# Three small moves in an attention and expert kernel: a row sum with its diagonals, a token list, and the last copy

## The chip, the cores and the metric

The kernel runs on one core of one Trainium2 chip. A core has TensorE (PE in the profile, with its weight loads as PEld), VectorE (DVE), ScalarE (ACT), GpSimd (POOL) and SyncE (SP); each works through its own queue of instructions in order, and they wait for one another by semaphores. TensorE writes its products to PSUM, a small memory in banks, from which VectorE and ScalarE read them. The metric is the device time of one execution in microseconds; the median over runs counts.

## The reference

First an attention block in the manner of RWKV5 (batch 4, 8 heads, 768 positions, head dimension 48), then a layer of 8 experts to which tokens are assigned greedily and in equal numbers.

```python
for t in range(S):
    kt, vt, rt = (k[:, :, t], v[:, :, t], r[:, :, t])
    cur = np.einsum('bhd,bhe->bhde', u[None] * kt, vt)
    y[:, :, t] = np.einsum('bhd,bhde->bhe', rt, state + cur)
    state = w[None, :, :, None] * state + np.einsum('bhd,bhe->bhde', kt, vt)
...
x = y.transpose(0, 2, 1, 3).reshape(3072, 384)
logits = x @ w_gate
for idx in np.argsort(-logits.flatten()):
    tok, e = idx // E, idx % E
    if assigned[tok] < 0 and counts[e] < 384:
        assigned[tok] = e
        counts[e] += 1
for e in range(E):
    out[assigned == e] = np.maximum(x[assigned == e] @ w1[e], 0) @ w2[e]
```

The weights of an expert are 384 x 1024 and 1024 x 384; everything is float32.

## The kernel before

**The attention** (class `Mild`) is cut into N = 24 units, four batches times six chunks of 128 positions; unit n is batch n mod 4, chunk n div 4. Its order is written out by hand in `Mild.run`, whose body for n finishes unit n and prepares the units after it; every engine receives its instructions in that order. For one unit the steps are these:

- `own(n)`: GpSimd multiplies r, k and u to `rk` (L442, L443).
- `own_sum(n)`: VectorE sums `rk` over the head dimension to `dd`, one number for a position and a head (L448).
- `turn(n)`: TensorE turns keys and r (L458); ScalarE copies the keys (`kT`, L475), VectorE scales r (`rT`, L477).
- `diagonal(n)`: ScalarE writes the eight heads' `AT` as the identity times `dd`, eight instructions at L495. They fill the diagonal and clear the rest.
- `pairs(n)`: TensorE multiplies `kT` by `rT` into the one buffer `g_ps` (L504); VectorE copies the part off the diagonal over `AT` with a mask, in two instructions, one for each half of the heads (L508). The buffer is free again after the second.
- `outputs(n)`: TensorE adds the state's part (`rT` by `states`) and the unit's own part (`AT` by `vts`) into the one buffer `y_ps` (L542); ScalarE copies it to `x` (L561).

In the body for n, `outputs(n)` and `pairs(n + 1)` belong to different units, and `diagonal(n + 2)` and `own_sum(n + 2)` to a third. Rows of x go back to memory by `rows_turned` (TensorE, L592; in the body for 23 it reuses the buffer of `g_ps`), `xr` (ScalarE, L601) and a transfer on SP's queue. In between, the steps of `walk.early` (names with `e_`) choose one expert, called the star, in advance from the chunks that are done, and list 256 of its tokens: `e_some`, `e_part`, `e_both` on VectorE, `list_ps` on TensorE (L1427), `e_tok` on VectorE, and then two gathers by GpSimd (L1515).

**The experts** (class `Experts`) follow, one after the other, numbers 0 (the star's first 256 tokens) to 8 (the star's last 128). For each, `walk` finds by search which expert fills next and which tokens it takes, `tokens` turns the places into a list of token numbers (VectorE makes `row`, `oh` and `vals`; TensorE six `some_ps`, L1409; VectorE `some`, `part`; TensorE `list_ps`, L1427; VectorE `mine`, `tok`), and `fetch` gathers rows and loads weights. The generator `later` holds this work, cut into slots by `yield`. `Experts.run` pulls the next slots at the progress marks in `due`: up to 1 is the first product of the expert, from 1 to 2 the second. Here a scheduler decides the final order, which is the same on every execution.

Some experts (3, 6 and 7) form the first product by seven smaller products P1 to P7 instead of eight (`hidden_by_seven`, L1598), in two passes. Sums of weights (`first_T`, L1545) and of rows (`first_S`, L1556) go in; VectorE adds `kept_P` to a product's bank (L1590), ScalarE keeps banks as `kept_P` (L1582) and writes `hid` (L1586). P6's bank is used again by P7 once ScalarE has kept it. Experts 6 and 7 form the second product by fifteen products (`p_ps`, L1726) from sums of `hid` and weights (`H`, `W`, L1670), with output sums on VectorE (L1735).

**The end.** Expert 8's output is a single block of 128 rows. `result` copies it from PSUM to `o_last` and its tokens to `tok_last`, since another arm of the program, which is not executed with these inputs, ends in the same tiles. After it each engine loads the flag `ok` (L975), branches (L1970), raises its count, and GpSimd scatters `o_last` to the output (L1747), called from the function's last line.

Of the kernel before, what the change touches and what calls it, by code (L numbers as in the profile page):

```python
# [274 lines left out]
class Mild:  # L275
# [340 lines left out]
    def run(self, step):  # L616
        N, B, C, walk = self.N, self.B, self.C, self.walk
        self.live = {n: {} for n in range(N)}
        self.start()
        u_ps = self.spread_u()  # L620
        self.again_one(0, 0)
        k0 = self.keys_turned(0, True)
        self.again_one(0, 1)
        self.idle(2, "g_ps")
        r0 = self.r_turned(0)
        self.copy_u(u_ps)
        self.own(0)
        self.scaled(0, "k", k0, "pieces")
        self.scaled(0, "r", r0, "pieces")
        self.table(self.WK, "k")  # L630
        self.again_one(1, 0)
        self.table(self.WR, "r")
        self.again_one(1, 1)
        self.idle(2, "g_ps")
        k1 = self.keys_turned(1, True, walk.ps, "few")
        wk_ps = self.wk_turned()
        r1 = self.r_turned(1, walk.ps, "counts")
        self.wk_table(wk_ps)
        self.scaled(1, "k", k1, self.WK)
        self.own_sum(0)  # L640
        self.diagonal(0, (0,))
        self.again_one(2, 0)
        self.diagonal(0, (1,))
        self.again_one(2, 1)
        self.scaled(1, "r", r1, self.WR)
        self.own(1)
        self.keys(0)
        self.own_sum(1)
        nc, AB = self.nc, self.ones8
        nc.vector.tensor_mul(self.chunk, AB[:, 0, :, 1, 8], AB[:, 0, :, 1, 8])  # L650
        self.pairs(0)
        self.diagonal(1)
        self.own(2)
        chores = walk.constants()
        for n in range(N):
            self.load(n + 5, "kr")
            self.load(n + 4, "v")
            if n == 2:
                self.gate_weights()
            soon, split, full = n <= B, 0 < n < 3, n >= B and n % B == 0  # L660
            halves = ((0,), (1,)) if split or full else ((0, 1), ())
            if n == 0:
                self.turn(2, True)
                self.own_sum(2)
                self.idle(3, "y_ps")
                self.pairs(1)
                self.keys(1)
            else:
                step(n, "first")
                if not soon and n + 3 < N:  # L670
                    self.again(n + 3)
                if n == 2:
                    self.own_sum(n + 2)
                if split:
                    self.keep(n - 1)
                    self.pairs(n + 1)
                if n + 2 < N:
                    if n != 2 and n + 3 < N:
                        self.own_sum(n + 2)
                    self.turn(n + 2, between=lambda: step(n, "turning"))  # L680
                if n <= N - B:
                    self.rows((n - 1,), "few")
            if soon:
                self.again_one(n + 3, 0)
            if n + 2 < N:
                self.diagonal(n + 2, halves[0])
            if soon:
                self.again_one(n + 3, 1)
            if n > 2:
                step(n, "turned")  # L690
                if n <= B:
                    self.keep(n - 1)
                if n + 1 < N:
                    self.pairs(n + 1, lambda: step(n, "products"))
                step(n, "paired")
            if n + 3 < N:
                self.keys(n + 3)
                self.own(n + 3)
                if n == 1:
                    self.keys(2)  # L700
            if full:
                self.gate(n // B - 1, range(B))
                if n + 2 < N:
                    self.diagonal(n + 2, halves[1])
            if n == N - 1:
                rows = self.rows_turned((N - 4, N - 3), "g_ps", lambda: step(n, "rows"))
                self.rows_out((N - 4, N - 3), rows)
            self.outputs(n, lambda: step(n, "states"), (lambda: self.logits(n // B - 1)) if full else (lambda: None))
            if split:
                self.diagonal(n + 2, halves[1])  # L710
            if n == N - 4:
                self.own_sum(N - 1)
            step(n, "last")
            if n == 13:
                walk.guess_most(self.LG[:, 0:3 * B, :], AX.XY)
            if n == 14:
                walk.guess(walk.ps.tile([128, 128], F32, name="most_ps", tag="few"), self.ident)
            if n == N // 2 + 1:
                for _ in chores:
                    pass  # L720
                self.test()
            if n > 2:
                for _ in range(6):
                    next(chores, None)
        self.gate(C - 1, range(B - 1))
        one = self.rows_turned((N - 2,), "kT_ps")
        self.gate(C - 1, [B - 1])
        last = self.rows_turned((N - 1,), "g_ps")
        self.logits(C - 1)
        return one, last  # L730
# [719 lines left out]
def rwkv5_eagle_then_base_layer_balanced(  # L1450
# [12 lines left out]
    nc = tc.nc  # L1463
    N, DX = out.shape
    E, _, F = moe_w1.shape
# [12 lines left out]
    walk = Assignment(ctx, tc, LG, CAP, C)  # L1478
    out_rows = dram_disjoint_views(out, NT)
    o_last = keep.tile([128, DX], F32, name="o_last")  # L1480
    tok_last = keep.tile([128, 1], I32, name="tok_last")
# [3 lines left out]
    class Experts:  # L1485
# [252 lines left out]

        def leave(self, o_sb, tok, to):
            if to is None:  # L1740
                nc.scalar.copy(o_last, o_sb)
                nc.vector.tensor_copy(tok_last, tok)
            else:
                self.scatter(o_sb, tok, to)

        def scatter(self, o_sb, tok, to):
            nc.gpsimd.indirect_dma_start(out=to, out_offset=bass.IndirectOffsetOnAxis(ap=tok, axis=0),  # L1747
# [2 lines left out]
        def result(self, c, hid, w2, tok, to):  # L1750
            o_ps = self.ps_o.tile([128, DX], F32, name="o_ps")
            for j in range(KF):
                nc.tensor.matmul(o_ps, hid[:, j, ts(c, 128)], w2[:, j, :], start=(j == 0), stop=(j == KF - 1))  # L1753
            if to is None:
                nc.scalar.copy(o_last, o_ps)
                nc.vector.tensor_copy(tok_last, tok[:, c:c + 1])
                return
            o_sb = self.o.tile([128, DX], F32, name="o_sb")
            nc.scalar.copy(o_sb, o_ps)
            self.scatter(o_sb, tok[:, c:c + 1], to)  # L1760
# [3 lines left out]
        def run(self, ahead, later, rows, pulls={}, xT=None):  # L1764
            xT, lead = xT or self.turn(ahead), True
            row_sums = weight_sums = None
            while ahead:
                n, _, tok, w1, w2 = ahead
# [8 lines left out]
                right = (self.fifteen_w2 if many else self.seven_w2)(w2) if whole and not late else None  # L1777
                left = {}
                some = pulls.get(n, 2)
                due = [1.55, 1.75] if some == 2 else [0.75 + 1.15 * i / (some - 1) for i in range(some)]  # L1780

                def half(hid):
                    nonlocal right
# [79 lines left out]
    with ExitStack() as whole:  # L1863
        x = Experts()
# [5 lines left out]
        with ExitStack() as part:  # L1870
# [20 lines left out]
            with tc.manual_schedule():  # L1891
# [18 lines left out]
                tok = walk.tokens(first["place"])  # L1910
# [15 lines left out]
                for m in (0, 1, 99):  # L1926
                    go(m)
                    xT = next(turned)
# [3 lines left out]
        def later():  # L1932
            yield from search
            walk.bound(ident)
            now = second
            for n in range(2, 5):
                walk.book(now, first=True)
                yield x.fetch(n, now["fmax"], walk.tokens(now["place"]))
                walk.leave(now)
                yield  # L1940
                now = walk.new_outs()
                yield from walk.likely_steps(**now)
            was = now
            walk.book(was)
            walk.leave(was)
            for n in range(5, E):
                rest = n == E - 1
                yield
                if rest:
                    yield  # L1950
                    now = walk.remainder()
                else:
                    now = walk.new_outs()
                    yield from walk.likely_steps(**now)
                walk.book(now, surely=rest)
                walk.choose(was, now)
                yield x.fetch(n, was["fmax"], walk.tokens(was["place"]))
                if not rest:
                    walk.leave(now)
                was = now  # L1960
            yield
            yield
            tc.mark_branch_hint_location("whole")
            have["ok"] = walk.found()
            yield x.fetch(E, walk.star, walk.tokens(walk.star_place, 1))

        x.run(ahead, later(), (a for a in [*out_rows[2:NT - 1], None]),
              {1: 5, 2: 7, 3: 9}, xT)

    with tc.If(have["ok"] < 1, label="whole", preferred_fallthrough_block=False):  # L1970
        with ExitStack() as arm:
# [2 lines left out]
        with ExitStack() as arm:  # L1974
            x = Experts()
# [40 lines left out]
```

## Time and profile before

| | us |
|---|---|
| median of 3 runs | 395.65 (395.48 to 396.61) |
| the profiled execution, its own time | 395.83 |
| its span, first to last instruction | 394.1 |
| TensorE's granted clock | 0.998 |

| engine | busy, us | share of the span |
|---|---|---|
| TensorE | 381.2 | 97% |
| VectorE | 281.3 | 71% |
| ScalarE | 169.1 | 43% |
| GpSimd | 141.0 | 36% |

The attention lasts until about 130 us, the experts from there to the end. In a line of the timeline the first number is the start in us from the span's start, the second the length (of several instructions, where it ends in xN with N over 1), then engine, line of the kernel, operation, output<-input, sizes. In square brackets stands how long the engine had been idle before it and what released it. A wait for several semaphores is put down to the one that came last by the profile, and that need not be the one that the program names.

### The profile page before, as it was taken

The page shows a single profiled execution, that of the slowest core. Times are in us where ns is not written, and L with a number is a line of the kernel's source. Part 1 is how long each engine was busy: PE and PEld are TensorE (multiplying, and loading weights), DVE is VectorE, ACT ScalarE, POOL GpSimd, SP SyncE. Part 2 cuts the span into 40 slices and gives each one's busy share as a digit, 9 for nine tenths or more (in the row PEclk, how much of TensorE's full clock was granted, in tenths as well). Part 3 has the DMA queues.
Part 4 walks back from the last instruction along what each step waited for, and adds up shares of the span by engine and source line. Part 5 has one row for each costly group of instructions (what it writes and reads, how often), then busy time and mean ns, then how long its engine had stood idle before and what let it go on. Part 6 is the DMA issues. An engine that isn't in the chain of part 4 may idle for free. (4 is left out here: it accounts for less than half of the span.)

```text
span 394.1 us, 9090 instructions
## 1 busy us (share of the span) xinstructions
PE 381.2 (97%) x3393; PEld 309.5 (79%) x3393; DVE 281.3 (71%) x959; ACT 169.1 (43%) x452; POOL 141.0 (36%) x173
## 2 busy tenths in 40 slices
PE   8999999999999999999999999999999999999993
PEld 7778888888887766677568799558756889989991
DVE  6855777576786778986859949978378976994530
ACT  4997878788883411222222242121222233234130
POOL 7888877656742013032121121202303202070020
PEclk9999999999999999999999999999999999999999
DMA  9999999987592155461470470109209265181010
GB/s 120 160 182 172 197 196 182 171 175 146 113 360 78 58 188 231 145 237 42 119 280 22 132 290 20 41 2 339 83 20 318 97 214 194 38 331 33 2 62 27
DMA packets 95332, 57.30 MB, mean 145 GB/s; under 512 B 77232, under 2 KB 89520, under 8 KB 95280
## 3 DMA queue, kind: packets, MB, share of 16 engines
q1 hardware_dynamic: 91936, 47.21, 47.7%
q0 software_dynamic: 3104, 9.44, 6.9%
q8 instruction: 28, 0.46, 0.5%
q14 instruction: 24, 0.20, 0.2%
q10 hardware_dynamic: 240, 0.00, 0.0%
HBM read 47.20 MB, written 9.44 MB: 144 GB/s over the span
## 5 line engine op out<-in xcount | busy, mean ns | idle before, releaser
L1621 PE MATMUL h_ps<-xT,w 128*128 128x384 f32 (+1 forms) x264 | 72.6, 427 | 0.0
L495 ACT ACTIVATE AT<-ident,dd 128x128 f32<-128x128 f32 x192 | 59.7, 394 | 1.2 <-DVE dd L448 1.1
L1621 PEld LDWEIGHTS h_ps<-xT,w 128*128 128x128 f32 x264 | 42.0, 191 | 19.6 <-issue 2.2
L1515 POOL DMA_INDIRECT xg<-x_rows,tok x22 | 22.2, 1008 | 92.3 <-PE h_ps L1621 23.7
L1747 POOL DMA_INDIRECT out_dram<-o_all,to x16 | 20.8, 1301 | 85.8 <-DVE o_all L1735 22.2
L508 DVE COPY_PREDICATED AT<-mask,g_ps 128x512 f32<-128x512 uint8 x48 | 32.7, 733 | 13.1 <-PE g_ps L504 11.5
L1624 ACT ACTIVATE hid<-h_ps 128x384 f32<-128x384 f32 (+1 forms) x40 | 17.9, 449 | 54.2 <-PE h_ps L1621 50.9
L1753 PE MATMUL o_ps<-w,hid 128*128 128x384 f32 x96 | 32.5, 490 | 0.0
L504 PE MATMUL g_ps<-rT,kT 48*128 48x128 f32 x384 | 27.9, 284 | 1.0 <-ACT x L561 0.6
L436 POOL TENSOR_TENSOR kss<-krs,wk 128x384 f32<-128x384 f32 x24 | 24.3, 1014 | 8.0 <-DVE krs L340 5.2
L504 PEld LDWEIGHTS g_ps<-rT,kT 48*128 48x128 f32 x384 | 23.4, 187 | 4.3 <-ACT AT L495 0.9
L1753 PEld LDWEIGHTS o_ps<-w,hid 128*128 128x128 f32 x96 | 17.7, 190 | 10.6 <-issue 0.5
L542 PE MATMUL y_ps<-AT,vts 128*64 128x128 f32 x384 | 25.7, 276 | 0.0
L443 POOL TENSOR_TENSOR rk<-rk,u_bc 128x384 f32<-128x384 f32 x24 | 24.2, 1009 | 1.9
L442 POOL TENSOR_TENSOR rk<-krs 128x384 f32<-128x384 f32 x24 | 24.5, 1019 | 0.2 <-DVE chunk L650 0.2
L542 PEld LDWEIGHTS y_ps<-AT,vts 128*64 128x64 f32 x384 | 20.6, 137 | 0.9 <-issue 0.3
L477 DVE TENSOR_TENSOR rT<-rT_ps,WR 112x512 f32<-112x512 f32 x23 | 15.8, 686 | 5.1 <-PE rT_ps L458 5.1
L561 ACT COPY x<-y_ps 128x512 f32<-128x512 f32 x24 | 14.1, 588 | 8.6 <-PE y_ps L542 8.6
L448 DVE TENSOR_REDUCE dd<-rk 128x8 f32<-128x384 f32 x24 | 13.1, 546 | 6.3 <-POOL rk L443 6.3
L458 PE MATMUL rT_ps<-ident,krs 128*112 128x128 f32 x96 | 15.5, 283 | 0.5 <-ACT krs L344 0.4
L1695 PE MATMUL pa_ps<-T,S 128*128 128x192 f32 x80 | 15.8, 331 | 0.0
L1726 PE MATMUL p_ps<-W,H 128*128 128x128 f32 x128 | 15.8, 275 | 0.0
(340 smaller groups left out, 831.3 us busy)
## 6 DMA issues: line engine op xcount, KB each, us to landing
w<-in_moe_w_dram SPq DMA_DIRECT2D x18, 1536.0 KB, 9.0
krs<-in_k_dram SPq DMA_DIRECT2D x24, 192.0 KB, 4.5
krs<-in_r_dram SPq DMA_DIRECT2D x24, 192.0 KB, 5.0
vts<-in_v_dram SPq DMA_DIRECT2D x24, 192.0 KB, 5.0
x_rows<-xr SPq DMA_DIRECT2D x24, 192.0 KB, 3.3
xg<-x_rows,tok POOLq DMA_INDIRECT x22, 4.0
out_dram<-o_all,to POOLq DMA_INDIRECT x16, 2.7
out_dram<-o_sb,to POOLq DMA_INDIRECT x5, 2.6
```

Source lines behind the costliest of these rows:

```text
L436: self.nc.gpsimd.tensor_mul(self.kss[:, n % self.NS].rearrange("p (g h) d -> p g h d", g=2)[:, :, :, 0:D], src, self.wk.rearrange("p (g h) ...
L442: nc.gpsimd.tensor_mul(rk, self.krs[:, n % self.NK, 1, 0:H, 0:D], self.krs[:, n % self.NK, 0, 0:H, 0:D])
L443: nc.gpsimd.tensor_mul(rk, rk, self.u_bc)
L495: nc.scalar.mul(AT[:, z, a, :], self.ident, dd[:, h:h + 1])
L504: nc.tensor.matmul(g_ps[:, z, a, :], kT[rows, a, :], rT[rows, a, :], start=True, stop=True)
L508: nc.vector.copy_predicated(out=AT[:, z], mask=self.mask.unsqueeze(1).to_broadcast([128, HP, T]), data=g_ps[:, z])
L542: nc.tensor.matmul(yv[q * PD:(q + 1) * PD, o // 2, o % 2, :], lhsT, rhs, start=(o // 2, q) not in seen, stop=stop, skip_group_check=True)
L1515: nc.gpsimd.indirect_dma_start(out=xg[:, c, :], out_offset=None, in_=x_dram[0:within, :], in_offset=bass.IndirectOffsetOnAxis(ap=tok[:, c: ...
L1621: nc.tensor.matmul(h_ps[j][:, at], w1[:, f, ts(j, 128)], xT[:, f, at], start=(f == 0), stop=(f == KD - 1))
L1624: nc.scalar.activation(hid[:, j, 0:m], h_ps[j][:, 0:m], AF.Relu)
L1747: nc.gpsimd.indirect_dma_start(out=to, out_offset=bass.IndirectOffsetOnAxis(ap=tok, axis=0), in_=o_sb, in_offset=None)
L1753: nc.tensor.matmul(o_ps, hid[:, j, ts(c, 128)], w2[:, j, :], start=(j == 0), stop=(j == KF - 1))
```

## The change

Three places.

- In the body for n = 21 (N - 3) the diagonals of unit 23 come after `outputs(21)` and no longer before `pairs(22)`, and unit 23's row sum comes after the masked copies of `pairs(22)` and no longer at the end of the body for 20.
- The star's list (`walk.star_place`) becomes a slot of its own, pulled in expert 6 at mark 0.4; its gather and weights are still fetched where they were in the program, at the start of expert 7.
- The last copy is cut at column 192 in two, the first half on ScalarE and the second on VectorE; `tok_last` is written first. The same is done in the arm that isn't executed.

```diff
@@ Mild.run
-            if n + 2 < N:
+            if n + 2 < N and n < N - 3:
                 self.diagonal(n + 2, halves[0])
...
                 if n + 1 < N:
                     self.pairs(n + 1, lambda: step(n, "products"))
+                if n == N - 3:
+                    self.own_sum(n + 2)
                 step(n, "paired")
...
-            if n == N - 4:
-                self.own_sum(N - 1)
+            if n == N - 3:
+                self.diagonal(n + 2)
             step(n, "last")
@@ Experts
         def leave(self, o_sb, tok, to):
             if to is None:
-                nc.scalar.copy(o_last, o_sb)
-                nc.vector.tensor_copy(tok_last, tok)
+                self.keep_last(o_sb, tok)
             else:
                 self.scatter(o_sb, tok, to)
+
+        def keep_last(self, o, tok):
+            half = DX // 2
+            nc.vector.tensor_copy(tok_last, tok)
+            nc.scalar.copy(o_last[:, 0:half], o[:, 0:half])
+            nc.vector.tensor_copy(o_last[:, half:DX], o[:, half:DX])
...
             if to is None:
-                nc.scalar.copy(o_last, o_ps)
-                nc.vector.tensor_copy(tok_last, tok[:, c:c + 1])
+                self.keep_last(o_ps, tok[:, c:c + 1])
                 return
...
-                due = [1.55, 1.75] if some == 2 else [0.75 + 1.15 * i / (some - 1) for i in range(some)]
+                due = [*some] if isinstance(some, tuple) else [1.55, 1.75] if some == 2 else [0.75 + 1.15 * i / (some - 1) for i in range(some)]
@@ later, and the call of run
+            star_tok = walk.tokens(walk.star_place, 1)
+            yield
             yield
             yield
             tc.mark_branch_hint_location("whole")
             have["ok"] = walk.found()
-            yield x.fetch(E, walk.star, walk.tokens(walk.star_place, 1))
+            yield x.fetch(E, walk.star, star_tok)
...
-              {1: 5, 2: 7, 3: 9}, xT)
+              {1: 5, 2: 7, 3: 9, E - 2: (0.4, 1.55, 1.75)}, xT)
```

In the built program the queues then differ in these places alone:

- VectorE: the row sum of unit 23 stands directly behind the masked copies of unit 22 (before: ahead of `e_some` of the star's first list and of those copies). The row, `oh` and `vals` steps of the last list stand where they stood; `some`, `part`, `mine`, `tok`, four steps that turn token numbers into output rows, and `tok_last` move from between the output sums and the W sums of expert 6 up to the place behind the same steps of expert 7's list, during expert 6's first product. There two W sums move up in their stead, and three `first_T` sums change places with `kept_P` sums. The second half of the last copy comes last.
- ScalarE: the copy of x of unit 21 stands ahead of unit 23's eight diagonals. The last copy is half as wide.
- TensorE: the last list's six `some_ps` and its `list_ps` move from the start of expert 7's first product to the middle of expert 6's.
- GpSimd: the gather of the last list's rows stands ahead of expert 6's three scatters.
- SyncE: the same order.
- Waits: unit 23's first masked copy waits for the fourth diagonal and the second for the eighth, as before. VectorE's half of the last copy waits for the count that ScalarE's half raises, and GpSimd's scatter for the counts of both engines.

## The prediction

> **What bounds the kernel now.** I read the page first, then the list of what TensorE waited for, then three stretches of the timeline.
>
> ```profile
> span 394.1 us, 9090 instructions
> PE 381.2 (97%) x3393; PEld 309.5 (79%) x3393; DVE 281.3 (71%) x959; ACT 169.1 (43%) x452; POOL 141.0 (36%) x173
> ```
>
> TensorE is busy for 97% of the span, so a part pays only if it shortens one of TensorE's waits, or the 6.9 us after its last product (394.1 - 387.2). The list of its waits has two that the change aims at, and both are small:
>
> ```profile
> PE g_ps L504 <- ACT x L561: 0.6, 1, 0.6
> PE list_ps L1427 <- DVE part L1418: 0.6, 1, 0.6
> ```
>
> All sums are made on the profiled execution (span 394.1, its own time 395.83) and carried to the median of 395.65, which lies 0.18 lower.
>
> **Part A: unit 23's row sum and diagonals.** The timeline of all engines from 115.9 on (start, length):
>
> ```profile
> 115.94 0.55 DVE L448 TENSOR_REDUCE dd<-rk 128x8 f32<-128x384 f32 x1 [1.21 <-POOL rk L443]
> ...
> 116.53 2.45 ACT L495 ACTIVATE AT<-ident,dd 128x128 f32<-128x128 f32 x8
> ...
> 118.37 1.34 DVE L508 COPY_PREDICATED AT<-mask,g_ps 128x512 f32<-128x512 uint8 x2
> 119.26 0.59 ACT L561 COPY x<-y_ps 128x512 f32<-128x512 f32 x1 [0.29 <-PE y_ps L542]
> ...
> 119.85 1.16 PE L504 MATMUL g_ps<-rT,kT 48*128 48x128 f32 x16 [0.64 <-ACT x L561]
> ...
> 121.12 1.34 DVE L508 COPY_PREDICATED AT<-mask,g_ps 128x512 f32<-128x512 uint8 x2
> ...
> 122.69 0.60 PE L592 MATMUL x_ps<-ident,x 112*128 112x112 f32 x4
> 122.80 0.17 DVE L933 TENSOR_TENSOR e_both<-e_part 128x8 f16<-128x8 f32 x1
> ...
> 123.12 0.17 PE L1427 MATMUL list_ps<-e_both,alike 128*128 128x8 f16 x1
> ```
>
> TensorE's wait at 119.85 is put down to x, but x began only when TensorE's own y_ps ended (119.20). In the program, g_ps of unit 23 waits for the masked copies of unit 22, which free its bank and end at 118.37+1.34 = 119.71. So moving x ahead of the diagonals releases nothing; moving the row sum does. e_some could start once its products end at 115.88, so at about 115.95 and not at 116.41: VectorE is 0.46 early until the masked copies, which end at 119.25. g_ps of unit 23 then starts at 119.40, a gain of 0.45.
>
> What is late next is unit 23's own masked copy. Its row sum (0.55) now stands behind unit 22's masked copies, from 119.14 to 119.69. The diagonals wait for it and for x (ScalarE is free 0.48 after x's start, as the kT copy after the x at 115.48 shows): they start at 119.75, and eight take 2.45, so the last ends at 122.20, and the fourth at about 121.0. The first masked copy (0.73 by its row) still starts near 121.13, since the row sum takes back the 0.46 and the small e_ steps between end as before. The second needs the last diagonal and starts at 122.23 where it started at 121.74 (121.12+1.34-0.72): +0.49. Queued behind it on VectorE are e_some, e_part and e_both (end 122.97, now 123.46); on TensorE x_ps, which reuses g_ps's bank, can't start before 122.23+0.72+0.14 = 123.09 (0.14 as from 119.71 to 119.85; before 122.69), and list_ps waits for e_both until 123.58 (before 123.12). Behind list_ps come e_tok, the two gathers of the first expert, whose second TensorE waits for at 129.36 (0.4), and the gate logits with the first list search. So TensorE's gain of 0.45 is spent waiting before x_ps, and everything from 123 on is **0.46 late**. Nothing later absorbs it: the remaining waits of TensorE (0.2 to 0.6 each) are for engines that this shift moves too. Bounds: -0.64 (the wait goes, nothing is late) to +0.65 (the row sum's 0.55 also delays the e_ steps by 0.1 to 0.2).
>
> **Part B: the last list a slot sooner.** The timeline around its old place, and VectorE's row that starts the stretch:
>
> ```profile
> 349.43 0.49 PE L1598 MATMUL hb_ps<-xT,w 128*128 128x192 f32 x2
> ...
> 350.51 0.18 PE L1427 MATMUL list_ps<-part,alike 128*128 128x4 f16 x1 [0.59 <-DVE part L1418]
> ...
> 351.76 0.54 DVE L1590 TENSOR_TENSOR kept_P<-kept_P,hc_ps 128x384 f32<-128x384 f32 x1
> ...
> 352.34 0.53 ACT L1586 ACTIVATE hid<-kept_P 128x384 f32<-128x384 f32 x1
> ...
> 352.77 0.87 ACT L1582 COPY kept_P<-h_ps 128x384 f32<-128x384 f32 x2
> ...
> 353.28 0.92 PE L1598 MATMUL h_ps<-first_S,first_T 128*128 128x192 f32 x4
> ```
>
> ```profile
> 332.89 0.69 DVE L1545 TENSOR_TENSOR first_T<-w,first_T 128x512 f32<-128x512 f32 x1 [0.31 <-PE h_ps L1598]
> ```
>
> A step of the 192-column products is 0.1625 (four in 0.81, eight in 1.46). From 349.43 to 350.96 four take 1.53 where 0.65 is due, so list_ps costs 0.88 there. The six some_ps cost 0.24 (347.24 to 348.13 for four products). Both go to expert 6, where the previous list shows the plain prices: 0.24, and 0.11 for a list_ps that waits for nothing (323.48 to 324.89 for eight). So 1.12 goes and 0.35 comes: -0.77 if TensorE alone were the bound.
>
> It isn't. At 353.28 the P7 products start just as ScalarE's first copy of L1582 ends (352.77 + 0.475): they need its bank. That copy is queued behind the hid at 352.34, which needs VectorE's sum at 351.76, and VectorE is full from 333.5 to there (by the windows 4.00 of 4 us from 336, 4.83 of 5 from 340, 5.00 of 5 from 345). This run starts where first_T at 332.89 waits for TensorE's h_ps. The seven products now stand before that point, so VectorE's run starts 0.35 later; four of the small list steps leave it (start to start 0.11, 0.09, 0.12 and 0.06: 0.38). P7 therefore starts at 353.28 + 0.35 - 0.38 = 353.25, and TensorE's wait has moved from list_ps to P7: **-0.03**. Bounds: -0.77 to +0.35 (the price paid, nothing returned). Hidden moves: list arithmetic and tok_last (eight steps of 0.15 to 0.2) fall into VectorE's 3.19 us wait for weights that ends at 329.11; uncovered they would cost about 1.4. The fourth gather follows three at GpSimd's 328.09 (1.0 each) and is over long before the three scatters that it passes (346.55 to 353.9); its rows are wanted at 373.4. The weights of the last list keep their place on SP's queue.
>
> **Part C: the last copy in two halves.**
>
> ```profile
> 387.27 0.48 ACT L1755 COPY o_last<-o_ps 128x384 f32<-128x384 f32 x1 [4.88 <-PE o_ps L1753]
> 388.19 0.97 POOL L1747 DMA_INDIRECT out_dram<-o_last,tok_last  x1 [7.51 <-ACTq L1970]
> ```
>
> In the built program VectorE's half waits for the count that ScalarE's half raises, so they follow each other. ScalarE's half is 0.32 (128x192 copies of L1700): 387.59. VectorE starts 0.03 later (377.23 to 377.26 for res) at 387.63. Then an engine loads ok, branches and raises its count: on ScalarE 387.27 to 387.92, 0.65, the copy's 0.48 lying beside the load of 0.47; on VectorE 378.60 to 379.36, 0.76, with a load of 0.55. GpSimd's scatter follows ScalarE's count by 0.28. So it starts at 387.63+0.76+0.28 = 388.67: **+0.48**, carried to the end, because all that is left there hangs on this scatter. Bounds: -0.16 (0.48 less 0.32, side by side and nothing else added) to +0.6. The Trainium skill speaks against this part: "PSUM - Partial Sum Buffer", section "PSUM bank collisions raise a hardware error", says that ScalarE and VectorE must not touch one bank on the same partitions at once, reads included. The halves share o_ps's bank; no run here shows a collision, but the wait in the program is what that rule asks for. By it the half is serial; without it VectorE would start at 387.27 and the scatter at 388.31, +0.12.
>
> **Sum:** +0.46 - 0.03 + 0.48 = +0.91, so 395.65 + 0.9 = **396.6** (the profiled execution: 396.7).
>
> **Rivals.**
> 1. *All three pay as meant.* For it: both waits are in the list. A -0.64, B -0.77, C -0.1: 395.65 - 1.5 = 394.1. Against: the second masked copy waits for diagonals that cannot start before the row sum's end, P7 for ScalarE. It needs slack that I don't see.
> 2. *The early list is paid for and nothing returns.* If P7's start follows VectorE's run without the 0.38 (the freed moments filled by the W sums that move up before hc's add), B costs +0.35, and the sum is 0.46+0.35+0.48 = 1.3: 396.95. It decides once the add of hc_ps starts more than 0.3 after 351.76, measured with A's shift taken off. For it: VectorE is full there; against: the W sums are as many.
> 3. *The diagonals stay covered.* A ends near 0 if x_ps and list_ps have room: then about +0.45, 396.1. Against: x_ps started without a gap after y_ps.
>
> **Chances.** I take 0.3% (1.19 us) as what a measurement can tell from no change. The main case has 0.60: its own range is 395.9 to 397.3 from mixed bounds, with 0.33 of it within the limit and 0.27 beyond 396.84. Rival 2 has 0.23 (0.20 slower), rival 1 0.08 (0.06 faster), rival 3 0.09 (0.08 within, 0.01 slower). Sum: faster 0.06, same 0.46, slower 0.48. The range for 8 in 10 is 395.7 to 397.7: from rival 3 less some scatter to all upper bounds (0.65+0.35+0.6 = 1.6) plus the 0.4 or so by which runs before differ.
>
> **What would show it.** A: g_ps of unit 23 about 0.45 earlier, then a wait of about 0.7 before x_ps, put down to VectorE, and e_tok near 124.0. B: no wait before list_ps, a new one of some tenths before P7's h_ps put down to ScalarE's L1582. C: VectorE's half starting after ScalarE's, the last scatter about 1.4 after TensorE's last product ends (before 0.96). I am wrong if x_ps follows y_ps without a gap, if P7 is more than 0.3 early against part A's shift, or if the two halves overlap.

## The result, and the profile after

| | before | after |
|---|---|---|
| median of 9 runs, us | 395.65 (395.42 to 396.61) | 397.1 (396.84 to 397.36) |
| the profiled execution, its own time | 395.83 | 397.03 |
| its span | 394.1 | 395.3 |

The ratio is 1.0033, with a 95% interval of 1.0023 to 1.0042: about 1.3 us slower, where the prediction had said 0.9.

The head of the page of the changed kernel, total busy time by engine:

```profile
span 395.3 us, 9093 instructions
PE 379.6 (96%) x3393; PEld 307.3 (78%) x3393; DVE 281.4 (71%) x960; ACT 168.8 (43%) x452; POOL 141.6 (36%) x173
```

TensorE issues as many products as before, so the loss is waiting, or lies behind its last product. The list of its waits (us in total, times, longest) shows two new ones in the stretches that were changed:

```profile
PE x_ps L592 <- DVE e_some L935: 0.8, 1, 0.8
...
PE h_ps L1600 <- ACT kept_P L1584: 0.6, 1, 0.6
```

The wait of 0.6 before list_ps and that of 0.6 before g_ps are gone, and these stand in their place. (Two more, 1.8 in total for the first loads of k and r before 12 us, are also in the profiles of part C alone and of the diagonals behind x; TensorE is 0.35 ahead of the profile of before when they are over, so they are no part of the loss.) The list puts the wait before x_ps down to e_some. But in the trace's records TensorE's separate wait instruction appears at 122.80, 0.04 after the masked copy ends (122.76, which frees the bank) and before e_some does (122.83): what ended the wait is the masked copy. The timeline of all engines shows all three parts (start, length; in brackets the idle time before and its releaser):

```profile
116.10 1.16 PE L504 MATMUL g_ps<-rT,kT 48*128 48x128 f32 x16
...
118.92 0.54 DVE L448 TENSOR_REDUCE dd<-rk 128x8 f32<-128x384 f32 x1
119.08 0.58 ACT L561 COPY x<-y_ps 128x512 f32<-128x512 f32 x1 [2.73 <-PE y_ps L542]
...
119.18 1.16 PE L504 MATMUL g_ps<-rT,kT 48*128 48x128 f32 x16 [0.16 <-PE y_ps L542]
119.56 2.45 ACT L495 ACTIVATE AT<-ident,dd 128x128 f32<-128x128 f32 x8
...
122.03 0.72 DVE L508 COPY_PREDICATED AT<-mask,g_ps 128x512 f32<-128x512 uint8 x1 [0.43 <-ACT AT L495]
...
122.91 0.57 PE L592 MATMUL x_ps<-ident,x 112*128 112x112 f32 x4 [0.81 <-DVE e_some L935]
...
351.99 0.54 DVE L1592 TENSOR_TENSOR kept_P<-kept_P,hc_ps 128x384 f32<-128x384 f32 x1
...
352.56 0.52 ACT L1588 ACTIVATE hid<-kept_P 128x384 f32<-128x384 f32 x1 [0.71 <-DVE kept_P L1592]
352.99 0.84 ACT L1584 COPY kept_P<-h_ps 128x384 f32<-128x384 f32 x2
...
353.51 0.92 PE L1600 MATMUL h_ps<-first_S,first_T 128*128 128x192 f32 x4 [0.60 <-ACT kept_P L1584]
...
387.49 0.32 ACT L1750 COPY o_last<-o_ps 128x192 f32<-128x192 f32 x1 [4.88 <-PE o_ps L1760]
387.84 0.36 DVE L1751 COPY o_last<-o_ps 128x192 f32<-128x192 f32 x1 [8.74 <-ACT o_last L1750]
389.39 0.97 POOL L1754 DMA_INDIRECT out_dram<-o_last,tok_last  x1 [8.49 <-DVEq L1978]
```

Read each part from a landmark inside it, since whole executions differ by some tenths. For part A it is g_ps of unit 22, in the profile of before this line:

```profile
116.29 1.16 PE L504 MATMUL g_ps<-rT,kT 48*128 48x128 f32 x16
```

- A, from the start of g_ps of unit 22: g_ps of unit 23 follows it by 3.08 (before 119.85 - 116.29 = 3.56), x_ps by 6.81 (before 122.69 - 116.29 = 6.40). The gain of 0.48 is there, and the wait before x_ps takes 0.89, nearly twice as much: +0.41.
- B: no wait before list_ps, but P7 (353.51) starts where ScalarE's first copy of L1584 ends, queued behind the hid that waits for VectorE's sum.
- C, from the start of the first copy: the scatter follows by 1.90, before by 388.19 - 387.27 = 0.92: +0.98.

### The profile page after: what moved, and what is told of

The parts are those of the page before. It is cut to its first block, busy times and chain, and to the rows that moved or that the text cites. A ratio compares the mean times of both kernels' runs of the same rounds, so it can differ in the third digit from the quotient of the medians.

```text
span 395.3 us, 9093 instructions
## 1 busy us (share of the span) xinstructions
PE 379.6 (96%) x3393; PEld 307.3 (78%) x3393; DVE 281.4 (71%) x960; ACT 168.8 (43%) x452; POOL 141.6 (36%) x173
```

## The experiments

The kernels ran in three sets, each on another chip and beside before. Before differed between the sets (medians 396.57, 395.43 and 396.63), so only ratios to before of the same set are compared. A step of 0.0001 in the ratio is 0.04 us.

| kernel | set | ratio to before, 95% interval | part's landmark against before |
|---|---|---|---|
| part A alone | 1 | 1.0010 (1.0001 to 1.0019) | +0.40 at x_ps |
| part B alone | 1 | 1.0003 (0.9995 to 1.0012) | +0.06 behind P7 |
| part C alone | 1 | 1.0014 (1.0005 to 1.0023) | +0.98 at the scatter |
| last copy whole on VectorE | 1 | 0.9999 (0.9989 to 1.0009) | +0.11 at the scatter |
| C, halves in the other order | 2 | 1.0013 (1.0004 to 1.0022) | +0.63 at the scatter |
| A, four diagonals on GpSimd | 2 | 1.0013 (1.0004 to 1.0022) | +0.46 at x_ps |
| B, copy of P6 ahead of the hid | 2 | 0.9985 (0.9976 to 0.9994) | -0.68 behind P7 |
| before, unit 23's rk early | 2 | 1.0011 (1.0002 to 1.0020) | +0.26 at x_ps |
| before, diagonals behind x | 3 | 1.0008 (0.9999 to 1.0017) | +0.40 at x_ps |
| before, copy of P6 ahead of the hid | 3 | 0.9999 (0.9989 to 1.0008) | -0.01 behind P7 |
| before, half of unit 23's rk early | 3 | 0.9987 (0.9978 to 0.9996) | -0.48 at x_ps |
| the three that pay | 3 | 0.9965 (0.9953 to 0.9977) | see below |

### The three parts alone

Each kernel is before with the lines of one part of the diff shown above.

> Only part A: row sum and diagonals of unit 23 moved. My theory: g_ps of unit 23 starts 0.4 to 0.5 us earlier than before, the second masked copy waits for the eighth diagonal, x_ps of the rows starts 0.4 us later with a wait of 0.6 to 0.8, and the time is +0.4 to +0.5 (396.1). Rival (the change's loss is in the other two parts, A is covered): within 0.1 of before (395.65). Rival (the moves pay): -0.4 to -0.6.

> Only part B: the last list a slot sooner. My theory from the trace of the whole change: no wait before list_ps, a new one of 0.5 to 0.6 before P7's h_ps put down to ScalarE's kept_P copy, and between -0.05 and +0.2 in all (395.6 to 395.85). Rival of the prediction (paid for and nothing returned): +0.35 or more (396.0). If TensorE alone were the bound: -0.77 (394.9).

> Only part C: the last copy in two halves. By the trace of the whole change the scatter starts 1.9 us after TensorE's last product ends (before 0.96), so +0.95 (396.6). By the prediction's sum, 1.4 us after it, +0.48 (396.1). If the halves had overlapped: 0.8 after it, -0.16.

A alone repeats its picture: x_ps follows g_ps of unit 22 by 6.80. B is read from the first h_ps of expert 6's first product (first line, before; second, part B alone) and from the products behind P7 (third line, part B alone; before 354.04):

```profile
317.81 0.90 PE L1598 MATMUL h_ps<-xT,w 128*128 128x192 f32 x4
...
318.05 0.90 PE L1598 MATMUL h_ps<-xT,w 128*128 128x192 f32 x4
...
354.33 1.14 PE L1598 MATMUL hb_ps<-first_S,w 128*128 128x192 f32 x6
```

TensorE was 0.23 behind the trace of before from 306 to 324 us and 0.29 behind from P7 on, so B costs 0.06; in the changed kernel the same two places give 0.05. C alone has the scatter 1.90 after the first copy's start. The parts add up: by the landmarks 0.40 + 0.06 + 0.98 = 1.44, by the ratios 0.0027, against 0.0033 for the whole. C's ratio alone is worth 0.2 to 0.9 us, a little less than the trace. A pause of TensorE may be the reason: the profiles of part A and of part B alone, whose ends are those of before, lose 0.4 near 381 us, and that of part C alone does not. If before loses it in this set too, C's time should be 0.98 - 0.4 = 0.58 longer, and 1.0014 is 0.56. Before was not profiled in this set, so that isn't shown.

### Part C: which wait is dear

The whole copy on VectorE (the diff is against part C alone, as the next):

```diff
-            nc.scalar.copy(o_last[:, 0:half], o[:, 0:half])
-            nc.vector.tensor_copy(o_last[:, half:DX], o[:, half:DX])
+            nc.vector.tensor_copy(o_last, o)
```

> Before, with the whole last copy on VectorE instead of ScalarE, and nothing split. GpSimd's scatter then waits for VectorE's count in the DMA instruction itself; in the changed kernel it waited for it in an instruction of its own ahead of the DMA. Theory 1 (the separate wait costs the 0.5 that the prediction lacked): the scatter follows VectorE's count by 0.28, so with copy start 387.27 and 0.76 to 0.8 to the count it starts 1.1 us after the last product's end, +0.1 to +0.2 (395.8). Theory 2 (VectorE's count takes longer to reach GpSimd, or VectorE's end is slower as such): about 0.8 after the count, 1.6 after the last product's end, +0.6 (396.3).

Its timeline:

```profile
387.67 0.56 DVE L1748 COPY o_last<-o_ps 128x384 f32<-128x384 f32 x1 [8.38 <-PE o_ps L1757]
388.70 0.97 POOL L1751 DMA_INDIRECT out_dram<-o_last,tok_last  x1 [7.63 <-DVEq L1973]
```

The scatter starts 1.03 after the copy does, 0.28 after VectorE's count ends (388.43 in the trace's records). That is theory 1: a count of VectorE reaches a waiting scatter as soon as one of ScalarE. The halves in the other order:

```diff
-            nc.scalar.copy(o_last[:, 0:half], o[:, 0:half])
-            nc.vector.tensor_copy(o_last[:, half:DX], o[:, half:DX])
+            nc.vector.tensor_copy(o_last[:, 0:half], o[:, 0:half])
+            nc.scalar.copy(o_last[:, half:DX], o[:, half:DX])
```

> Part C alone with the order of its halves turned: VectorE copies the first half, ScalarE the second behind it. GpSimd then meets VectorE's count in the instruction ahead of the scatter, and the scatter itself waits for ScalarE's, which comes last. Theory 1 (the DMA is prepared during its own wait, but not during the wait ahead of it): VectorE's count 0.84 after the last product's end, 0.75 from there to the scatter, and ScalarE's way (0.04 + 0.39 + 0.65 + 0.28) gives 1.36; the later one decides, so the scatter starts 1.55 to 1.65 after the last product's end (before 0.96, part C alone 1.94), +0.6 to +0.7. Theory 2 (VectorE's end is slow as such, whoever is last): 1.9. The prediction's own arithmetic: 1.36 to 1.4.

Its timeline, and then its chain that ended last (start, length, what):

```profile
386.87 0.36 DVE L1748 COPY o_last<-o_ps 128x192 f32<-128x192 f32 x1 [8.38 <-PE o_ps L1758]
387.26 0.32 ACT L1749 COPY o_last<-o_ps 128x192 f32<-128x192 f32 x1 [5.28 <-DVE o_last L1748]
388.42 0.97 POOL L1752 DMA_INDIRECT out_dram<-o_last,tok_last  x1 [8.15 <-ACTq L1974]
```

```profile
387.63 0.03 POOLq L1752
387.66 0.53 issue
388.20 1.19 POOLq L2015
```

The page puts the scatter's idle time down to ScalarE, whose count was up at 387.91. The chain shows what decided: GpSimd's separate wait for VectorE ended at 387.66, and the scatter started 0.76 later. By ScalarE's count alone it would have started at 387.91 + 0.28 = 388.19. This is theory 1 again. The changed kernel has the same end in its chain:

```profile
388.60 0.03 POOLq L1754
388.63 0.53 issue
389.17 1.19 POOLq L2019
```

388.63 to 389.39 is again 0.76. A scatter that waits for a count itself follows it by 0.28, whether ScalarE or VectorE raised it; one that stands behind a separate wait instruction follows the end of that by 0.76. Part C made GpSimd wait for two engines, and the later one stood in the separate instruction.

### Part A: what is late, and what it would take

Only the diagonals moved, the row sum at its old place:

```diff
-            if n + 2 < N:
+            if n + 2 < N and n < N - 3:
                 self.diagonal(n + 2, halves[0])
...
+            if n == N - 3:
+                self.diagonal(n + 2)
```

> One half of part A alone: unit 23's diagonals behind the copy of x of unit 21, the row sum at its old place. My theory (A's loss is that the diagonals start only behind x, the row sum's place sets only the gain): g_ps of unit 23 starts as before, the eighth diagonal ends some 3 us later than before, the second masked copy waits for it and x_ps is 0.4 to 0.5 late, so +0.4 to +0.5, as part A alone. Rival (the diagonals are late because the row sum is): with the sum at its old place they are in time, and the time is that of before. The prediction's sentence, that moving x releases nothing for TensorE, is tested with it: g_ps of unit 23 not earlier.

```profile
115.63 0.55 DVE L448 TENSOR_REDUCE dd<-rk 128x8 f32<-128x384 f32 x1 [1.22 <-POOL rk L443]
...
118.94 0.58 ACT L561 COPY x<-y_ps 128x512 f32<-128x512 f32 x1 [2.72 <-PE y_ps L542]
119.42 2.44 ACT L495 ACTIVATE AT<-ident,dd 128x128 f32<-128x128 f32 x8
119.53 1.16 PE L504 MATMUL g_ps<-rT,kT 48*128 48x128 f32 x16 [0.65 <-ACT x L561]
...
121.90 0.73 DVE L508 COPY_PREDICATED AT<-mask,g_ps 128x512 f32<-128x512 uint8 x1 [0.37 <-ACT AT L495]
...
122.77 0.57 PE L592 MATMUL x_ps<-ident,x 112*128 112x112 f32 x4 [0.34 <-DVE e_some L935]
```

This timeline has dd ready at 116.2 and still ends 6.80 behind g_ps of unit 22 (115.97) at x_ps, as part A does. g_ps of unit 23 is not earlier (3.56), though the bracket names x as its releaser. So the diagonals' place costs what A loses; the row sum's place gives g_ps its 0.48, which the same wait swallows. The ratio's interval just reaches no change; the trace decides here.

Four of the eight diagonals on GpSimd, in part A:

```diff
-                self.diagonal(n + 2)
+                self.diagonal(n + 2, (0, 1), nc.gpsimd.tensor_scalar_mul)
...
-                nc.scalar.mul(AT[:, z, a, :], self.ident, dd[:, h:h + 1])
+                (other if other and z else nc.scalar.mul)(AT[:, z, a, :], self.ident, dd[:, h:h + 1])
```

> Part A alone, with four of unit 23's eight diagonals on GpSimd (idle there for 8 us) beside the other four on ScalarE. My theory (A's loss is the wait for the eighth diagonal): the second masked copy follows the first without a wait, about 0.45 earlier than in part A alone, TensorE's wait before x_ps shrinks from 0.8 to 0.3 to 0.4, and the time falls back to that of before (0.0 +- 0.1), not below it, since VectorE's sum of steps up to the masked copy is unchanged. Rival (the loss comes from x_ps waiting for the bank whatever the diagonals do): still +0.4. Rival (the move pays once the diagonals are covered): -0.4.

```profile
119.88 2.36 POOL L495 TENSOR_SCALAR AT<-ident,dd 128x128 f32<-128x128 f32 x4 [3.97 <-ACT x L561]
...
120.55 0.44 DVE L935 TENSOR_TENSOR e_row<-e_lo,iota 128x128 f16<-128x128 int32 x1
...
122.27 0.73 DVE L508 COPY_PREDICATED AT<-mask,g_ps 128x512 f32<-128x512 uint8 x1 [0.15 <-POOL AT L495]
```

A miss: GpSimd took 0.6 for each, and VectorE's steps beside it slowed (e_row 0.44, before 0.29), so that the masked copy was late again. As a test of the cause it says nothing.

Next, the gain without the diagonals' move. In before, VectorE idles for 1.21 ahead of the row sum, waiting for GpSimd's rk. Both of GpSimd's products a body sooner:

```diff
-                self.own(n + 3)
+                if n + 3 < N - 1:
+                    self.own(n + 3)
+                if n + 3 == N - 2:
+                    self.own(N - 1)
```

> Before, with nothing of the change, but GpSimd makes unit 23's rk a body sooner (in its idle 2.7 us ahead of the states), so that the row sum finds it ready and lies in VectorE's 1.2 us of idle time. Row sum and diagonals stay where they were. If VectorE's row of steps from there to the masked copies is what sets the pace, g_ps of unit 23, x_ps, the list and everything behind are 0.4 to 0.5 early: -0.45 (395.2). If TensorE or a gather sets it, g_ps starts early and the gain is waited away before x_ps or before the gathered rows: 0.

```profile
110.68 1.00 POOL L443 TENSOR_TENSOR rk<-rk,u_bc 128x384 f32<-128x384 f32 x1
110.83 1.40 DVE L936 TENSOR_TENSOR e_row<-e_lo,iota 128x512 f16<-128x512 int32 x1
```

e_row took 1.40, before 0.67. VectorE lost 0.73 there, and only then won 0.47. GpSimd's first product stood beside a masked copy that kept its 1.35. So only that one was moved, and the second took the first one's old place (the new `own_u` holds it):

```diff
-                self.own(n + 3)
+                if n + 3 < N - 1:
+                    self.own(n + 3)
+                else:
+                    self.own_u(N - 1)
+                if n + 3 == N - 2:
+                    self.own(N - 1)
```

> Before, with nothing of the change, but of GpSimd's two products for unit 23's rk only the first made a body sooner (beside VectorE's masked copy, which did not slow in the run with both sooner); the second takes the place of the first. With both sooner, VectorE's e_row beside the second took 1.40 instead of 0.67 and lost 0.74, and the row sum's move then gained 0.47. My theory: e_row stays at 0.67, the row sum lies in VectorE's idle time, and g_ps of unit 23 and what follows are 0.4 to 0.47 early: -0.4 (395.2). Rival (VectorE slows beside any GpSimd product): 0 to +0.3.

```profile
110.83 0.68 DVE L943 TENSOR_TENSOR e_row<-e_lo,iota 128x512 f16<-128x512 int32 x1
...
113.83 1.01 POOL L449 TENSOR_TENSOR rk<-rk,u_bc 128x384 f32<-128x384 f32 x1
114.87 0.55 DVE L453 TENSOR_REDUCE dd<-rk 128x8 f32<-128x384 f32 x1
...
119.39 1.16 PE L509 MATMUL g_ps<-rT,kT 48*128 48x128 f32 x16 [0.17 <-DVE e_upto L1179]
...
122.22 0.60 PE L597 MATMUL x_ps<-ident,x 112*128 112x112 f32 x4
```

e_row is at 0.68, the row sum lies in the idle time, and x_ps follows g_ps of unit 22 (116.30) by 5.92, before 6.40. The ratio of 0.9987 lies wholly below 1. This is the gain that part A was after.

### Part B: the wait behind the hid

ScalarE's copy of P6's bank ahead of the hid that waits for VectorE's sum, with part B and without it (`held` keeps the hid's arguments until then):

```diff
-                    keep(p, name, ps)
+                    kept_ins = keep(p, name, ps)
+                    if name == "P6" and p == 0:
+                        with tc.issue_after(kept_ins.ins):
+                            block(*held.pop())
```

> Part B alone, with ScalarE's copy of P6's bank put ahead of the hid that waits for VectorE's sum (in all experts that use the seven products). My theory (the gain of B sits in P7's wait behind that hid): the wait of 0.6 before P7's h_ps goes, and TensorE is 0.5 to 0.7 ahead of part B alone, so -0.4 to -0.6 against before (395.1). Rival (VectorE's full stretch is the bound, the wait only moves to the next of its sums): a new wait of similar size within 5 us behind P7, and -0.1 to +0.2 against before.

> Before, with nothing of the change, but ScalarE's copy of P6's bank ahead of the hid, in all experts with seven products. Theory 1 (the two belong together: the early list frees TensorE, the copy's place lets it use that): only the small waits for that copy go, 0.18 in expert 7 and about 0.1 in each of experts 3 and 6, so -0.2 to -0.4 (part B with it measured -0.6). Theory 2 (the place of the copy is worth the whole, the early list nothing): -0.6.

The timeline of part B with it:

```profile
350.70 0.81 PE L1602 MATMUL h_ps<-first_S,first_T 128*128 128x192 f32 x4
...
351.61 0.48 ACT L1582 COPY kept_P<-h_ps 128x384 f32<-128x384 f32 x1 [0.17 <-PE h_ps L1602]
352.14 0.92 PE L1602 MATMUL h_ps<-first_S,first_T 128*128 128x192 f32 x4
352.16 0.52 ACT L1587 ACTIVATE hid<-kept_P 128x384 f32<-128x384 f32 x1
```

The copy follows P6 at once, P7 starts as the copy ends, and TensorE's list has no h_ps wait any more. TensorE goes from 0.14 ahead of before (306 to 322 us) to 0.82 ahead behind P7, so it gains 0.68, of which 0.10 comes at the same copy in expert 6 (323 us). Without the early list the same edit gives nothing that can be measured (0.41 behind before at 306, 0.40 behind after P7): it wins the 0.10 in expert 6 and loses 0.09 in expert 7, less than both theories said. Part B alone costs 0.06, the copy's place alone gives 0.01, and together they give 0.68. So the wait before list_ps and the one before P7 were in series, and each hid the other.

### The three that pay

Before, with part B, the copy ahead of the hid, and half of rk early:

> Before with the early list (part B), the copy of P6's bank ahead of the hid, and the first product of unit 23's rk a body sooner; the last copy and the diagonals as before. If the parts add: -0.6 and -0.4, so -1.0 (394.65). If waits for gathers and weights take part of it: -0.5 to -0.8.

395.48 against 396.63 in the same set, ratio 0.9965 (0.9953 to 0.9977). It beats before, and the changed kernel's ratio was 1.0033. By the landmarks the parts add up to 0.48 + 0.68 = 1.16; the times give 0.9 to 1.9. In its profile another 0.43 is lost at the end: the scatter before the last took 4.36 to land (2.82 in before), GpSimd so left its last wait only at 387.48, and the last scatter followed 0.75 later (388.23), 1.35 after the copy began instead of 0.92.

## Why the prediction was right, and where it was not

The prediction gave 0.48 to slower by more than 0.3% and 0.46 to no change, and 397.1 lies in its range. By the landmarks the sum was short by 0.5 (0.91 against 1.44), nearly all in term C. C lies outside its own bounds (-0.16 to +0.6). That the total lies in the range all the same is owed to the range's width: its upper end adds all three upper bounds, and A and B stayed 0.24 and 0.29 below theirs.

- **A, +0.46: measured +0.40 to +0.41.** Every step held: x moves nothing, g_ps of unit 23 0.48 early (0.45 forecast), the second masked copy behind the eighth diagonal, x_ps late. The diagonals moved alone show it. "Nothing later absorbs it" holds as far as the ratios can tell.
- **B, -0.03: measured +0.06 alone.** The mechanism was right: the wait moved to P7, behind ScalarE's L1582, fed by VectorE. Expert 6 paid 0.35 for the list's products, as forecast, but a later h_ps lost another 0.10: `first_T` sums now stand ahead of `kept_P` sums, which I listed and did not price, and in part B alone this h_ps (331.97) starts as the delayed `kept_P` sum ends (331.37 + 0.55). VectorE's full stretch so began 0.45 later, not 0.35. Of this it gave back 0.40 (0.38 forecast).
- **C, +0.48: measured +0.98.** The halves were serial, 0.35 apart, as foreseen. "PSUM - Partial Sum Buffer" of the Trainium skill, section "PSUM bank collisions raise a hardware error", asks for a semaphore between two engines at one bank; no run here let them touch the bank together. VectorE's way to its count was 0.75 (0.76 forecast). The step that failed is the last: "GpSimd's scatter follows ScalarE's count by 0.28". That row is of a scatter that waits itself. In the changed kernel the late count is met by a separate instruction, and 0.79 passes from the count to the scatter. The bound of +0.6 was too low for the same reason. The trace of before had the right row: its gathers behind a separate wait start 0.74 after it (198.29 to 199.03, and four more alike).
- **The rivals.** Rival 2 names 396.95, near the result, but by another road: its sign was an add of hc_ps more than 0.3 late, and that was 0.05. Rival 1 fell with both new waits, rival 3 with the wait before x_ps.

## What to carry to other kernels

When an instruction gets a second engine to wait for, look in the built program which of the waits it keeps itself and which goes to an instruction ahead of it: here the late one must be its own, or a scatter starts half a microsecond later. A wait that is taken away pays only when the next in line has room; ask which queue that next one stands in, and change its order in the same step. And to fill an engine's idle time, move what it waits for rather than its own work, beside neighbours that don't slow.

## What the hardware showed unexpectedly

- GpSimd's indirect transfers, with nothing else under way on it, start 0.27 to 0.28 after a count that they wait for themselves, and 0.74 to 0.76 after a separate wait instruction ahead of them.
- VectorE slows beside GpSimd by instruction: e_row (int32 in, f16 out) from 0.67 to 1.40 beside a 128x384 product of 1.00, while masked copies from PSUM kept 1.34 to 1.35 beside the same. GpSimd took 0.6 for a 128x128 product by a column beside VectorE's small steps.
- TensorE makes pauses that no edit explains, and they go by the set. All eight profiles of sets 1 and 3 lose 0.61 to 0.68 against the profile of before between 125.3 and 127 us, and the six of them whose end is that of before lose another 0.37 to 0.42 near 381 us. The four profiles of set 2 and that of the changed kernel lose neither. The two pauses make about 1.05, and before is 1.1 to 1.2 slower in sets 1 and 3 than in set 2; where the pauses come from is open. Sums of half a microsecond can't be read from two spans; they can from landmarks close together.
